# A written-out order of instructions made anew: TensorE's instruction blocks assumed to be needed later, four steps of the first chunk with other durations

## Chip, core and metric

The kernel runs on one core of a Trainium2 chip. The metric is device time in microseconds (us) of one execution, the median over runs. The profile comes from one execution, recorded by the hardware profiler; its span runs from the first to the last instruction.

## What is computed

A delta-rule attention, a recurrence over 768 positions for 4 x 8 heads of width 48, feeds a SwiGLU feed-forward layer after an RMS norm.

```python
for t in range(S):                      # S = 768, head_dim D = 48, B = 4, H = 8
    kt, vt, bt = k_n[:, :, t], v[:, :, t], beta[:, :, t, None]
    y[:, :, t] = einsum('bhd,bhde->bhe', q[:, :, t], state)
    v_old = einsum('bhde,bhd->bhe', state, kt)
    state = state + bt * einsum('bhd,bhe->bhde', kt, vt - v_old)

x = y.transpose(0, 2, 1, 3).reshape(B * S, H * D)      # 3072 tokens of 384
xn = x / sqrt(mean(x * x) + 1e-6) * rms_g
g, val = xn @ w_gate, xn @ w_val                       # 384 -> 1536
out = (silu(g) * val) @ w_out                          # 1536 -> 384
```

k_n is k divided by its norm. The weights arrive as 64-bit floats and are made into 32-bit ones on the chip.

## The kernel before

**Chunks.** The sequence is cut into 12 chunks of 64 positions (C = 64); a chunk holds 256 tokens, since all four batches go together. In a chunk the recurrence becomes dense algebra: scores of k against k, the inverse of a triangular matrix, products with the state, and an update of the state. `norms` (L604 to L632) takes the norms of k; `prep` builds the scores and the inverse, for chunks 0 and 1 in `invert` with small triangular solves on VectorE and TensorE (L701 to L882); `recur` (L1212 to L1283) solves for u, reads the output y, takes its RMS norm (for chunk 0: squares L1308, mean L1326, power L1333, products L1344 and L1348), transposes it (L1371) and multiplies it by g (L1376, L1380); the state follows from L1283. The feed-forward layer of chunks 0 and 1 is `ffn_plain`: products with w_gate and w_val at L1443, Silu at L1451, the product with it at L1452, and w_out at L1425. From chunk 2 on, `ffn` and `down` use factored products (L1538, L1595) with fewer multiplications.

**Weights.** `weights` loads 18 pieces of 768 KB each; two ScalarE steps (L500, L501) and two VectorE steps (L495, L498) make each piece into 32-bit floats. The first feed-forward products need the first pieces.

**An order written out.** Each step is recorded by `P.add(engine, duration, ...)` with what it reads and writes. `ORDER` is a long string that encodes the order in which all steps are emitted, found beforehand by a search over a model. `Plan.run` (L232) decodes it, calls `Plan.times` (L154), which gives every step a start, and emits the steps in this order. Each engine then runs its own steps in that order, whatever the real times are; semaphores keep the data right. The order on SP, the queue that issues nearly all DMAs, comes out of the same string.

**Fillers.** The model's starts have one direct effect on the program: where TensorE is expected to sit idle for over 0.8 us before 110 us, `fillers` (L104) puts in products of the identity matrix that nobody reads, of 512, 256 or 128 columns (emitted at L1714). A filler is four instructions, as is any other 32-bit product (two weight loads and two matmuls); a transpose is two.

**Instruction blocks in the model.** `times` counts TensorE's instructions. The tuple `PACKET` has three numbers: `first`, `each` and `reach` (L164). The block of number k is taken to be asked for when the count reaches first + each * k, and to be needed when it reaches that plus `reach`:

```python
first, each, reach = PACKET
...
    a, b = first + each * len(asked), first + each * used + reach
    if a >= more and b >= more:
        break
```

`fetch` (L167) gives the time at which a block is there: a lag of 4.2 us, and more when DMAs are queued. A step in which a needed block isn't there ends later by what is missing. In the kernel the numbers touch nothing else: no instruction waits because of them.

**Around the change.** In chunk 0 TensorE runs L560 (transposes of k and q), L701 (scores), L583, L842, L875, L842, L1212, L1236, L1190, L1371, L1283 and then the feed-forward layer, in this order, with fillers in between. Groups that go through 64 small products (L701, L583, L842, L875, L1212, L1236, L1190, L1283, L1113, L1128, L1176) hold 128 instructions each, except where halves are named.

Of the kernel before, what the change touches and what calls it, by code (L numbers as in the profile page):

```python
# [16 lines left out]
C = 64  # L17
W = 32
# [3 lines left out]
PACKET = (130.2, 254.45, 314.0)  # L22
# [10 lines left out]
    "#.#'#-#z#&###R#+#)#,#S#(#/#*#4#3#0#H#a#W#>#_#b#`#X#m#Y#%$:#Z#$#C$;#n#p#T#o#c#q#U#V#v#f#M#d#[#w#e#x#u#^$g#I$<#y$=#{#s"  # L33
    "#|#g#~#}#h#r#1$##t#2$$#?$l#E$%$&#]$)$($'$*$>$+#J%L$-$,#D$/$.#N#K$0#L#@%O$3#O$q$4#P%z$5$?#F$@#Q$m$7$A$6%M$B#G&$$n$o#="
    "%P$C#;#i%N#l#j$r#9#A$E#k$D$G$F$h$H$b$t$I$v$p$J$K$j%Q#8$T$L#B$M$U%y$i$V$O$W$N$1%$%[$X$Y$P%U$Z$Q$S$8$[$]$R$^%R%V&7$9${"
    "%W%S$k$d&C&8%T$s%X$c$_%)$u&9&;%Y%Z&:$e&<%](%$f&?%{#6&=%^$a&>&@%_%`$2$`%a$w&E%|'$$}%b$x&&%c&A%3&F'%%%&%%}%d#5&D&G&B%~"
    "'&&'%f&I&(%&&H$|%'&J%e%h%8$~&K%#%=%.%g%5%(&{&L&)$y%+%k&M&#%*&~&N'B%l%m%j%B%9&O%4%,%i'C&S&|%-'E$z%:%n%;%>&T&}%p%/%o%<"
    "'F%s%@%?&U%u'Q'?&*%q%6(&%t&X%r'#'D%0%A%v%G%1#7&P%2%w%x'G&Q%C&R'''H'I&Y&V'K&W('%7'J&Z'L'+%D'M&_#:((&[%H#<()&`'(')'*&]"
    "%J(*','N&a%I&+'<'R'-&b&d'.'@(z'0({&e'/'A%E(+'1'O&i%K'>'2)_&j&f&g&,&1'4%F(-&k&n'3&2'=(,)b'P*B&^'S)`&c'T'U)a&5)c'V'8&3"
    "'W&o'9'5'X':'6';)d'7'Y'Z)<)f'[)e&h&p)i'])j&m&l&4'^&6&r)h'_)g&s&q'`(6'a'b(:'c(;'d'e(7(.'f)l)k&t)+(8(<'g(9(=(/)>&x)8)?"  # L40
    "'j'h(>(|'k&u'i(}(?),)-(D(@(0(~(E's(1'u)='r(B(C(A(F'v)#)n'q)m(I'y)o'x't(G)@(J'n)p'l'p(N)q)r(K'w)s'm'z'o)t*A(O)u'{*H(L"
    ")v'|&z(P(S(2)w($*I(#'})x'~(H&y(4)y)B)z(M(Q){(3*C(X)|)A)D(Y)C*D(T*E)})~)E*F(U(Z*#*$(R(V*%,q)$(^*&(5([*G&w)](c*')F)G(_"
    ",*)H*(**(d*)).)^*+,-)/,+,p)9(W,,(`,.)0+d*7(e(a)I*0)%,/*5)&)J*1(h)'*9,0(f*3,1)1*4(i)L+f,4,<*J*8(m)K*,)2,3):,5(n,2*2)3"
    ")Q*.)M+e*6)R(])4)N*/)O)S)((j*-)P*:)T)5,7*K)6,6*;,=,x)U)V*<)W&-*L(b*?)X(o(k*=,w)Y*@+g)7*>)Z*P))+j)**N(g)[+k,8&v(p,r*M"
    ",9*R,:+h,;,>(l*S,?,s,@,A,B*T,C(q,D*U,t,E&.,F(r,u,G*V,H(s,I,J*X(w*W(t*Z+i,v(u*Y*_.Y(v*[(x*a*`*e,K.Z(y*},L*f.[+#*b*g,M"
    "*c*k.],N*h*]*i+l*d*l+$*m*^*j,O*u*n*q.^*v*Q+%,P*w+m,Q+&*x*r*~+),R*s._,S+'/G+n,T*t*O+-+o*o+(,U*y+.+/+*.`*z+5,X+0*{,V+3"
    "*p+6,W*|,y+q+7,Y+4+;/F+8.a+1+9+p+++?+r+:,b.b,),f+<+t,e+s,z+@,c+=.c,g+,);+G.d,h+A.f+C+>.e+H+y.g+D+u+z+O.h+2+v+w,],(+x"
    "+E,d,{+{+I,_+B+|.6,[+}+F+~,|,i.j+Q+J,Z+M,j,a.7+P.o,`,#+K,^.p,k.i+L-#+U,$,l+W,},o,m.8,n&/,%.9+N+X.<,&.:+R,'+S.k.l-$.m"
    "/H.n.q,~-%.r+T.s.;/N.t-'.u+V/I.>.v+[.=.w/J.x.y/K.?.z.{+]+Y.|-&+_&0.}+^-+/L.W10-)+Z.@.A+`-*.~-(11.B12/#--1z+a.C-,+c-1"
    "+b.D-.-3-213.E-7.X.F/M/$-9-8.G/%-/-O-:/&-=14-4-Q/'-5-;->-S-0-<.H/(-G-T-6-?15-H-C/)-I-R.I-J-[/*-P-D-W/+-@-U-E16-]/,-K"  # L50
    "-V-d-X/--L-Y-^//-F-M.J-Z-b17/00i/.-N-_1y-c18/O-e-f-A/91:-B.K19-h/:-g1=-j-`-i/1-n-a/8-z/=/P-k/>-o1>-l-r1E1<-{1;/Q-v1F"
    "/<-s/4-~-w/5-t-p/S-m-x-u/;-q.L/?1?.$1@-y.M0j/7.N-|.#/6.O.*/2/@.(/3.P/T0k.Q-}.R.S.&2$.T.).U.+.%1A/A/R1B..1C/D1D/E1G/C"
    "/B1H.'1I1J0o1K1L0l1M0q0p1N.,1{1O0m.V./0n1P.1/W.01|/U0r1}/X1Q1R1~/Y.-1S.2/Z1T/V1U/[.32#.5/^0s/].43c1//`/_0&0t1V3d0v/d"
    "3e0u/a/f4O/e0w/j1W/l/g/k3f1X0x0(2%/b/m1Y0*0y/c0z/p1Z0+/n1[3g/q/r/o1]/h/z2&1^/v0{/i/{1_020)3h/|2'/}1b/w0.0'0|/s/x1`0,"
    "031./~/y3i0-0:0/1c0#041a0;00080$1l051m0@0%1i093j0}0</t061o0>/u1k010=1f2)3k1q0A1p0?3?1e3l2(1n3m0D0~3@0B073n0H0E3o3p1r"
    "0F0I3q0L0P4P0J1s0C0T3x1d0M1h1#0N0O1t1$3r0G1%0K3B1&1j1v1g1'1w1(1u0V3s1)1x3A3y1*0R0U1+0Q4W0Z0S0]2*4V1,3E1-0[0^0X0W3t3F"
    "3u4Q3v3w3z0a3{0Y3|3}3~4R4#2.4$0b4S0d4%202/4&4T224'210_4(4)244*264U0`2X69230e254+6:0c272:6;0f4,0h2@0g2;2<4-6<2B2A4.2,"
    "2F2C2=2Z2G2>3C2D4/6=2P402E3G2-2H2?282Q2]412R3D2L2I2[293H6>2S2^422+2Y432_443I2M2a453J2N2`2T6?3L3K2O2e462b3M482U2g492f"
    "2V2k3N2h3O2m6@2J3P2o472W2K7&6A2l4X2n4>2p2q4B6B2w6C3Q2r6D2s2x6N6G2{6E2t2i6F2c3#3a6O4C2j2|4Y3R2y2u3$4F2}3+4E2~3%2d4G2v"
    "6I2z3'3S3-3(3,6H3&3)4D3*3b314[4Z333T3/4=347'3.4@6J4H4<306K5r4_6L3U4I6M326P4;4J6Q4A5t3V6R354?5s6S6T4N4:4K6U3W3X6V4L7."  # L60
    "3Y4M373Z6W6X366Y5x3[3]5u3^6Z3;7(383_5z3`6[4a7)3<5v3=4c7*5y4b4`6]5w4e3:4d7+4]6^5{4f6_4g6`4m4h4^4i7,5|9X8l5}5/3>4n5~39"
    "4o4j6#6a8m4u6$7-4p4s9Y6b516c4t4w6%6d8o4v4y6&6e4x536'4z4k4q8n4{6f4l6g5'684r54678p5#6h525(5;6(5$5)575*6k7/506j5+5%4|55"
    "8q5,4}6l705<6)5&568H6i715=588r5C5>5A4~5?8I6*5-5D5E5.596s5B5I5:6v5F5@6r5G8s6x6z5M5H6y6p8t5N6+5J6n5Q8v5Y6w8u6u5U729%5R"
    "8w6{5V5O8y5^5S8x5P5W5T8z6|5Z5K6m5L6o6}6,6q5`6t5X6-5[6.8J9&8|8{5_5d7#6/7$607%616~625]8K5e5g8N638L5a645b658P5f9Z668}5j"
    "8~5c9#9$9'9(779)9*5k9+8O5m9,799[78739-8M7;9]9`7:9.5h9/5l9^9a9075917=745i928Q7<93945n9_</957C5o8R;B5p8S7?5q7D8T7b7>8U"
    ";C7@7K768V967A7I7L977E7J988W7d8X;E7F7O8Y997G;D7M7P7f9:7N7Y9;;F7B7Q7H<07g7Z7U7e8Z9<7[7n7]9=7R7j7c7V9>;G7o7h7W9b7v9?7i"
    "7^8[8k9A7p7X7k;H9c7_7l9B7q7`7t7S9d8]7w7x7a9f7T7u9@7|7y9I;I7r7z9M9J8$7{8^;J7}9K9N8%8(8j9O;L9e9P;K8,9D8)7~9E848*;N8-;W"
    "9L8_;O8&;X8+;P9Q7m;M8':{8`7s8.9H8a8/9R9F:~808b9h8#9S9G:}8c9C86819W;R9T8d9V;Q82858e9U:|8:838<8f8g;%8h8i8=9j88<1;S8;;T"
    ";U8@;V<2;Y;Z87;[;]89;^;_9l8A;&;`9k8C8><38B;#;a9m;b;'<4;c;$9n;d9p8?;e;(9o;f<58D;)=u;*;@;+9q9r8E;g;,8G9v=v9s;-9x8F9w;/"
    "9|;h;.9~;0;i9}:8=x;j:#:&<79y:(;k9z:$:';19{=w::;l:%=y9t:0:):;9u:,:1;2:<9i:2:-:*:@;m:==z:3:4;n:99g:D:+:.;3:5:>:/:6;o:g"  # L70
    ":?;p={:7:E;q:A:F:J:G;u:L;A;s:K:B=|:N;t:H;4:P<8:O;r:M=}:I:Q:V=~<&>#<':Z:W>$:R:C:[>%:_:c>&:]:X>':S<9;~;5:T<#>.=Q;x:^:U"
    ":h:Y<(:`:i>(:d:a;6>):b;7;v:e;8>/;|;9:m<6:j<):f;:;;;{;<<>;=:k:n:p<$;z;>:o:s:l<%;?<:>*;}<;<<>+>,<@>->0=S>1:t:q>2<A:u>3"
    ">4>5>6<*>7<F<=<.:r>8;w<B=R;y>9<D:v>::w>c<E>;<-<,<+<G<C<L:x><:y<H:z<M=W<I>==T=Y>><R=U>?<T<S<N=X<U>@=V=Z>A<O<k=[<P=]<X"
    ">B=^<V=_<Y<Z<J>C=`<Q<c<K=a>D<m<W<d=b<o=s<e=c<n<_<f<?<p<[>b<l<s>E<`<q>F<g>G<r=d<w=t<h<y>K<x<i<a>I?y<t<]<b=e<u<z<}>H<v"
    "<^=%<j<~=#<{=&='=$=f=->X=(>Y=)=.=1>d=/=g=5?z>J=*===0=+=6=2>Z=h=3>e<|>[=4=7>U=i=,?|>S=j=8=k=;>V=>=?=l>P=m=9>W>T=:>N=n"
# [181 lines left out]
def kernel(  # L257
# [17 lines left out]
    nc = tc.nc  # L275

    B, H, S, D = q.shape
# [116 lines left out]
    P = Plan()  # L394
    V = lambda n: 0.13 + 0.0011 * n
    VF = lambda n: 0.13 + 0.0006 * n
    A = lambda n: 0.2 + 0.0008 * n
    G = lambda n: 0.15 + 0.0022 * n
# [1351 lines left out]
```

## Time and profile before

| | us |
|---|---|
| median of 3 runs | 656.71 (656.12 to 658.66) |
| the profiled execution | 654.99 |
| its span | 653.2 |
| TensorE matmul busy | 645.3 (99%) |
| VectorE busy | 540.7 (83%) |
| ScalarE busy | 300.2 (46%) |
| fillers L1714: 70 matmuls | 22.25 from their starts to the next starts |

PE is TensorE's matmul side and PEld its weight loads, which overlap; DVE is VectorE, ACT ScalarE, POOL GpSimd. In the timeline a row merges equal instructions in a row: start, duration, engine, line, operation, tiles, count, and in brackets the idle time before it and what ended it. "issue" stands for time in which the engine waited for nothing that the profile shows. In a table by stretches, the number in brackets behind an engine's busy time counts its instructions. The queue q8 of the DMA table carries TensorE's instructions.

### The profile page before, as it was taken

Reading aid. Unit: us, or ns where it says so; the run is one execution under the profiler, and the core shown is the slowest. Engines: PE = TensorE matmul, PEld = TensorE weight load, DVE = VectorE, ACT = ScalarE, POOL = GpSimd, SP = SyncE. Lnnn points to the kernel's source line nnn. Section 1 sums busy time; section 2 is a strip of 40 time slices with the busy share of each in tenths; the row PEclk is TensorE's granted clock in tenths of the full one; section 3 lists DMA queues with packets and bytes.
Section 4 is the critical chain, followed back from the end, with each engine's and each line's share of the span. In section 5 each row is a group of like instructions: output and inputs, shape, how many; then the busy total and the mean of one; then the engine's idle time right before and its main releaser. Section 6 shows DMA issues by size and latency. Waiting matters only on the chain.

```text
span 653.2 us, 23284 instructions
## 1 busy us (share of the span) xinstructions
PE 645.3 (99%) x9976; PEld 595.5 (91%) x9976; DVE 540.7 (83%) x1143; ACT 300.2 (46%) x712; POOL 137.5 (21%) x201
## 2 busy tenths in 40 slices
PE   8999999999999999999999999999999999999997
PEld 5688887788899999999999999999999999999997
DVE  6989889999899899789798798898798888558363
ACT  5778752325256344345254445345354254243231
POOL 4112250031510510510611320620510410000000
PEclk9999999999999999999999999999999999999999
DMA  9987764556656576285268385375174523111101
GB/s 213 249 241 222 216 144 71 93 84 121 145 89 99 141 142 103 51 152 114 51 107 150 53 159 102 68 153 92 47 141 80 98 59 65 21 39 25 25 1 25
DMA packets 270583, 69.36 MB, mean 106 GB/s; under 512 B 257488, under 2 KB 262736, under 8 KB 270160
## 3 DMA queue, kind: packets, MB, share of 16 engines
q1 hardware_dynamic: 269360, 67.63, 51.3%
q8 instruction: 78, 1.28, 0.8%
q10 hardware_dynamic: 1120, 0.25, 0.2%
q14 instruction: 25, 0.20, 0.1%
HBM read 49.76 MB, written 22.02 MB: 110 GB/s over the span
## 4 chain that ended last, share of the span: by engine, by line
PE 91%; SPq 3%; DMA 2%; DVE 2%; issue 1%; POOL 1%; ACT 0%; POOLq 0%; DVEq 0%; ACTq 0%
PE bank L1538 40%; PE bank L1595 20%; PE bank L1443 10%; PE bank L1425 5%; PE bank L583 3%; SPq L402 3%; PE bank L1113 3%; PE bank L1714 2%; PE bank L1190 2%; PE bank L1176 1%; PE bank L1283 1%; PE bank L1055 1%; PE bank L1075 1%; PE bank L560 1%; DMA at<-dkk 1%
## 5 line engine op out<-in xcount | busy, mean ns | idle before, releaser
L1538 PE MATMUL bank<-xf,w_in 128*128 128x128 f32 x1440 | 179.0, 276 | 0.5 <-issue 0.5
L1538 PEld LDWEIGHTS bank<-xf,w_in 128*128 128x128 f32 x1440 | 169.9, 192 | 2.1 <-issue 0.7
L1548 DVE TENSOR_TENSOR tmp<-tmp,bank 128x512 f32<-128x512 f32 x180 | 119.6, 682 | 42.9 <-PE bank L1538 33.1
L1538 PE MATMUL bank<-xf,more 128*128 128x128 f32 x960 | 124.1, 276 | 0.0
L1538 PEld LDWEIGHTS bank<-xf,more 128*128 128x128 f32 x960 | 115.4, 192 | 1.2 <-DVE tmp L1604 0.2
L1550 ACT COPY tmp<-bank 128x512 f32<-128x512 f32 x120 | 69.0, 585 | 92.3 <-PE bank L1538 53.2
L1554 ACT ACTIVATE tmp<-tmp 128x256 f32<-128x256 f32 x120 | 48.1, 416 | 63.7 <-DVE tmp L1548 63.4
L1006 DVE TENSOR_REDUCE acc<-acc 128x30 f32<-128x90 f32 (+4 forms) x150 | 71.0, 473 | 5.2
L1595 PE MATMUL bank<-wo_sb,hf 128*128 128x192 f32 x360 | 64.2, 330 | 0.0
L1000 DVE TENSOR_TENSOR acc<-acc,at 128x60 f32<-128x60 f32 (+4 forms) x150 | 53.2, 355 | 8.6 <-POOL at L980 5.5
L1595 PEld LDWEIGHTS bank<-wo_sb,hf 128*128 128x128 f32 x360 | 57.9, 190 | 1.2 <-issue 0.4
L945 POOL TENSOR_TENSOR at<-at,beta_b 128x256 f32<-128x256 f32 (+3 forms) x32 | 21.1, 693 | 156.0 <-DMA at<-dkk 156.0
L1555 DVE TENSOR_TENSOR hf<-tmp 128x256 f32<-128x256 f32 x120 | 47.1, 419 | 1.4 <-ACT tmp L1554 1.3
L628 POOL TENSOR_TENSOR knrm<-ksum,half 128x16 f32<-128x16 f32 x11 | 32.3, 2938 | 61.5 <-DVE ksum L607 61.5
L1026 POOL COPY acc<-acc 128x128 f32<-128x128 f32 x40 | 16.9, 453 | 84.5 <-DVE acc L1006 83.8
L1425 PE MATMUL bank<-wo_sb,hf 128*128 128x384 f32 x96 | 34.7, 493 | 0.0
L1443 PE MATMUL bank<-xp,w_in 128*128 128x256 f32 x144 | 34.1, 386 | 0.0
L1443 PE MATMUL bank<-xf,w_in 128*128 128x256 f32 x144 | 32.8, 382 | 0.0
L1395 DVE TENSOR_TENSOR xf<-xf 128x256 f32<-128x256 f32 (+1 forms) x70 | 28.1, 421 | 4.2 <-ACT xf L1365 3.8
L1443 PEld LDWEIGHTS bank<-xf,w_in 128*128 128x128 f32 x144 | 27.0, 190 | 4.8 <-issue 0.2
L1443 PEld LDWEIGHTS bank<-xp,w_in 128*128 128x128 f32 x144 | 26.5, 190 | 4.5 <-DVE xp L1376 0.3
L1425 PEld LDWEIGHTS bank<-wo_sb,hf 128*128 128x128 f32 x96 | 17.1, 190 | 8.4 <-issue 0.2
(221 smaller groups left out, 978.4 us busy)
## 6 DMA issues: line engine op xcount, KB each, us to landing
at<-dkk SPq DMA_DIRECT2D x20, 256.0 KB, 3.9
vt<-in_v_dram SPq DMA_DIRECT2D x24, 192.0 KB, 4.2
k<-in_k_dram SPq DMA_DIRECT2D x23, 192.0 KB, 4.5
out_dram<-tmp SPq DMA_DIRECT2D x46, 96.0 KB, 2.2
dks<-k SPq DMA_DIRECT2D x14, 256.0 KB, 3.4
kt<-dks SPq DMA_DIRECT2D x28, 128.0 KB, 3.2
more<-in_moe_w_gate_dram SPq DMA_DIRECT2D x4, 768.0 KB, 9.7
more<-in_moe_w_out_dram SPq DMA_DIRECT2D x4, 768.0 KB
```

Source lines behind the costliest of these rows:

```text
L628: P.add("POOL", 2.95, lambda: nc.gpsimd.tensor_tensor(out=knrm[i2], in0=ksum[i2], in1=half, op=ALU.pow), pn, r=[("ksum", i2), "half"], w=[ ...
L1000: nc.vector.tensor_tensor(out=acc[:, 1:3, 0:n, j + 2 : W].rearrange("p a i t -> p i a t"), in0=acc[:, old, 0:n, j : j + 2, None].to_broadc ...
L1006: nc.vector.tensor_reduce(out=acc[:, new, 0:n, j + 2 : W], in_=acc[:, lo : lo + 3, 0:n, j + 2 : W].rearrange("p a i t -> p i t a"), axis=A ...
L1395: P.add("DVE", V(128 * n), lambda dst=dst, a=a, b_=b_, op=op: nc.vector.tensor_tensor(out=dst, in0=a, in1=b_, op=op), pxv, r=[("xp", 0), ( ...
L1425: nc.tensor.matmul(po[p].t[:, 0:DM], hf[:, spot(f), 128 * p : 128 * p + 128], wo_sb[:, spot(f)], start=(f == f0), stop=(f == f1 - 1), skip ...
L1443: nc.tensor.matmul(ps.t[:, TOK * side : TOK * side + TOK], w_in[:, side, h_, 3 * t + i_, n : n + 128], x_[:, 2 * t : 2 * t + 2].rearrange( ...
L1538: nc.tensor.matmul(g.t[:, 128 * z : 128 * z + 128], fac[:, side, 128 * f : 128 * f + 128], xf[:, xs], start=(begin and z == 0), stop=False ...
L1548: P.add("DVE", V(512), lambda t=t, g=g: nc.vector.tensor_tensor(out=t, in0=t, in1=g.t, op=ALU.add), -1, r=[g], w=[tk], last=g)
L1550: P.add("ACT", A(512), lambda t=t, g=g: nc.scalar.copy(t, g.t), -1, r=[g], w=[tk], last=g)
L1554: P.add("ACT", A(256), lambda t=t: nc.scalar.activation(out=t[:, 0:256], in_=t[:, 0:256], func=ACTF.Silu), -1, w=[tk])
L1555: P.add("DVE", V(256), lambda t=t, f0=f0, p=p: nc.vector.tensor_tensor(out=hf[:, spot(f0) : spot(f0) + 2, 128 * p : 128 * p + 128], in0=t[ ...
L1595: nc.tensor.matmul(g.t[:, 0:192], a_[:, f], b_[:, f], start=(begin and f == 0), stop=(f == 5), skip_group_check=True)
```

## The change

Three edits. `reach` in `PACKET` goes from 314 to 444 instructions. In `recur`, four durations that the model uses for chunk 0 change: the squares of y (0.53 to 0.36), the scaled copy of half of y on VectorE (V(192), which is 0.34, to 0.42), and the two copies of the transposed y times g (V(128), 0.27, to 0.36 on VectorE; A(128), 0.30, to 0.37 on ScalarE). And `ORDER` is another string of the same length, so that all engines' orders, the DMAs' and the fillers change; no step is added or left out besides fillers, which go from 35 to 22.

```diff
-PACKET = (130.2, 254.45, 314.0)
+PACKET = (130.2, 254.45, 444.0)
...
 ORDER = (
-    "#.#'#-#z#&###R#+#)#,#S#(#/#*#4#3#0#H#a#W#>#_#b#`#X#m#Y#%$:#Z#$#C$;#n#p#T#o#c#q#U#V#v#f#M#d#[#w#e#x#u#^$g#I$<#y$=#{#s"
...
+    "#.#+#-#$#&###'#R#z#S#)#(#0#*#3#4#/#H#a#W#>#_#b#`#X#m#Y#,$:#Z#M$;#p#n#T#q#o#U#V#v#d#2#c#[#w#f#C#^#x#J#y#{#I#1#|#g$<#~"
...
 )
...
-                        P.add("ACT", 0.53, lambda p=p, g=g: nc.scalar.activation(
+                        P.add("ACT", 0.36, lambda p=p, g=g: nc.scalar.activation(
                             out=yn[:, p, 192 * g : 192 * g + 192], in_=psy[g, p].t[:, 192 * p : 192 * p + 192], func=ACTF.Square,
...
-                            P.add("DVE", V(192), lambda p=p, dst=dst, src=src: nc.vector.tensor_scalar(
+                            P.add("DVE", 0.42, lambda p=p, dst=dst, src=src: nc.vector.tensor_scalar(
...
-                        P.add("DVE", V(128), lambda p=p, psx=psx: nc.vector.tensor_scalar(
+                        P.add("DVE", 0.36, lambda p=p, psx=psx: nc.vector.tensor_scalar(
                             out=xdst[:, 2 + p], in0=psx.t[:, 128:256], scalar1=g_sb[:, 1:2], scalar2=None, op0=ALU.mult,
                         ), pxv, r=[psx, "g"], w=[(xkeys[p], 1)], last=psx)
                         continue
-                    P.add("ACT", A(128), lambda p=p, psx=psx, k_=k_: nc.scalar.mul(
+                    P.add("ACT", 0.37, lambda p=p, psx=psx, k_=k_: nc.scalar.mul(
```

What the new order moves on TensorE, by the built programs (counts are of its instructions, from the first filler on):

| | before | after |
|---|---|---|
| between L842 and L875 of chunk 0 | 3 fillers | 4 transposes of k (L560) |
| between L1212 and L1236 | 3 fillers, L560, 3 fillers | 2 fillers |
| between L1236 and L1190 | 3 fillers | none |
| between L1190 and L701 of chunk 1 | 3 fillers | none |
| between L701 and L1371 | L560 | L560, 3 fillers |
| between L1371 and the first L1443 | L560 | L1283, L560 |
| three 64-product groups with nothing between, counts | none | L1236, L1190, L701 at 944 to 1328; L875, L1128, L583 at 2352 to 2736; L1176, L583, L1113 at 5064 to 5448; L1113, L583, L1113 at 6436 to 6820; L1176, L1113, L1190 at 18364 to 18748 |

On POOL, the four instructions that make mask_p (L418, L421) come ahead of those that make the identity matrix. On SP, the two loads of v for chunk 0 stand between the first weight pieces instead of behind most of them, and the two loads of q for chunk 1 move ahead of loads of k, v and beta that they followed.

## The prediction

> **What bounds the kernel now.** I read the busy shares first, then who waited for whom on TensorE.
>
> ```profile
> PE 645.3 (99%) x9976; PEld 595.5 (91%) x9976; DVE 540.7 (83%) x1143; ACT 300.2 (46%) x712; POOL 137.5 (21%) x201
> q8 instruction: 78, 1.28, 0.8%
> ```
>
> TensorE (PE) is busy 99% of the span. Its instructions arrive on q8: 78 blocks, 1.28 MB, so 16.4 KB and 256 instructions each (2 x 9976 / 78).
>
> ```profile
> PE bank L1714 <- POOL ident masks.py:199: 1.4, 1, 1.4
> PE bank L669 <- DMA tmp<-in_beta_dram: 0.7, 1, 0.7
> PE bank L1714 <- issue: 0.5, 1, 0.5
> PE bank L560 <- DMA k<-in_k_dram: 0.5, 1, 0.5
> PE bank L1538 <- issue: 0.5, 1, 0.5
> ```
>
> Each line of this list of waits has a total, a number of times and the longest, in us. All data waits lie before 41 us. From the first feed-forward product on, PE never waits for data until the tail, so every us that its front takes less, and every us that it then stands still, shows in the time. Two waits are "issue", with no releaser. Where do they lie? The table by stretches, cut just before each resumes, counts the instructions that had run:
>
> ```profile
> 0.00:30.60 30.60, 27.27 (x477) 18.12 (x477) 24.07 (x70) 19.99 (x48) 8.99 (x12) 1.00 0.95 236
> 0.00:374.30 374.30, 370.14 (x6201) 326.14 (x6202) 328.94 (x710) 187.12 (x439) 96.68 (x134) 1.00 0.64 133
> ```
>
> 477 + 477 = 954 and 6201 + 6202 = 12403. The model with reach 314 puts the need of block 2 at 130.2 + 2 x 254.45 + 314 = 953.1 and of block 47 at 12403.4. Both stalls stand on a block's first instruction, to within one. With 444 the needs would be 1083 and 12533, where nothing happens. So **the trace contradicts the new number**; a program laid out by it stalls where its model sees nothing.
>
> Now the front, where the gain could be:
>
> ```profile
> 28.60 1.15 PE L1212 MATMUL bank<-vt,mt 64*64 64x48 f32 x64 [0.22 <-DVE vt L1155]
> 29.68 0.48 PE L1714 MATMUL bank<-ident 128*128 128x256 f32 x1
> 30.69 0.93 PE L1714 MATMUL bank<-ident 128*128 128x256 f32 x5 [0.52 <-issue]
> 31.45 0.60 PE L560 MATMUL bank<-ident,k 128*128 128x128 f32 x4
> 31.89 1.47 PE L1714 MATMUL bank<-ident 128*128 128x512 f32 x6
> 33.28 1.55 PE L1236 MATMUL bank<-u,kk 64*32 64x48 f32 x64
> ...
> 35.84 1.24 PE L1190 MATMUL bank<-u,pt 64*64 64x48 f32 x64
> ...
> 40.09 1.10 PE L1371 MATMUL bank<-ident,yn 128*128 128x128 f32 x6
> 41.03 0.60 PE L560 MATMUL bank<-ident,q 128*128 128x128 f32 x4
> 41.65 3.07 PE L1443 MATMUL bank<-xp,w_in 128*128 128x256 f32 x12
> 44.65 1.15 PE L1283 MATMUL bank<-u,k 64*64 64x48 f32 x64
> ```
>
> ```profile
> 30.39 0.47 ACT L1226 COPY u<-bank 128x384 f32<-128x384 f32 x1
> ```
>
> L1236 needs the copies of u, and the last ends at 30.86. It starts at 33.28: the fillers and the L560 ahead of it held it up by 2.2 us.
>
> **The change, part by part** (minus is a gain). The four durations and `reach` enter the model alone; they cost nothing but through the order.
>
> *Start.* On POOL, mask_p now precedes the identity: L418 and L421 take 0.15 and 0.79 us, with gaps 1.0. PE's first fillers start that much later; 0.52 us of it is covered by the wait for k ahead of the first L560, so the chain through L701 and VectorE's inverse starts 0.5 late. Further on, one L495 (start to start 0.47) has moved behind L1155, which releases L1212: L1212 starts at 28.6, as before. Sum 0.
>
> *From L1212 to the first L1443.* Two fillers (1.1 us) end at 30.8, u is copied by then, L1236 goes at 31.05: 2.2 earlier. L1190 follows 2.6 later, as before, at 33.6; L1371 4.3 after that, since the squares, mean, power and products between are the same, at 37.9; L1371 takes 1.1, L1283 1.1 (now ahead), L560 0.6: the first L1443 at 40.7. Before, it was 41.65 with L1283 still to do, so 42.7 for the same work: **-2.0**. Ends: -2.6, if squares and products start as early as u allows; 0, if VectorE, which by then has done two L495 and one L710 less (1.6 us), passes its arrears on.
>
> *VectorE behind it.*
>
> ```profile
> 50.00:60.00 10.00, 10.00 (x162) 7.97 (x161) 9.65 (x26) 8.66 (x17) 2.91 (x1) 1.00 0.63 159
> 60.00:70.00 10.00, 10.00 (x224) 7.95 (x223) 9.89 (x19) 7.50 (x11) 2.96 (x2) 1.00 0.97 340
> ```
>
> DVE is busy 9.65 and 9.89 of 10 us while it feeds chunk 0's products and chunk 1's inverse. A PE that is 2 us ahead meets a DVE that is 0.4 ahead (2.0 less the arrears). I take **+0.8**, half of the difference, as other products stand in between; ends 0 and 2.
>
> *Blocks.* A block is asked for 314 instructions ahead of its need. In this trace a block lands 2.05 us (fastest) to 8.6 after that, median 3.1, and the two stalls ended 1.4 and 1.5 after the landing, so it is usable 3.5 us after asking at the least, 4.5 at the median. A 64-product group takes 1.07 us for its 128 instructions (L1283 to L1443: 44.65 to 45.73), so 314 such in a row take 2.6: too short by 0.9 at least. The old order has one stretch between asking and need whose instructions alone run under 4.9 us: that of block 2, which stalled. The new order has eight:
>
> - block 9 (2420 to 2734: L875, L1128, L583): 2.6 us. DMAs are many there; blocks 8 to 10 were usable after 6.9, 4.0 and 3.9. I take 4.2: **+1.6**, ends 0.9 and 4.3.
> - block 25 (6491 to 6805: L1113, L583, L1113): 2.6. Blocks asked for in such groups past 110 us mostly come after 3.6: **+1.0**, ends 0.9 and 2.5.
> - blocks 72, 63 and 59: 3.4, 3.8 and 4.4: **+0.7** together, ends 0.1 and 3.
> - block 4 (asked for in L1190 at 34.35, needed in L1283 at 39.9): 5.5 us, against 7.0 that it took before, with SP sending four loads at 31 to 35: **+0.8**, ends 0 and 1.5. Blocks 2 and 3 have 4.8 and 5.5 us with the waits in their stretches, and few DMAs by then: 0, ends 0 and 1.
> - block 47 stalled before because it landed 4.7 us after asking; its stretch is 5.4 us of work now (5.6 before), enough for a median block: **-0.6**, ends -0.7 and 0; block 2's stall is in the front's term.
>
> Here the Trainium skill speaks for the change: "Runtime: NRT & Kernel Launch", section "Instruction fetch mechanics", has instructions streamed in 16 KiB blocks of 256, which agrees with the 16.4 KB above, and says that the fetch is hidden, because instructions are issued more slowly than blocks fill. The two waits at 954 and 12403 disagree; by that rule the block terms would be 0 and the sum -1.2.
>
> **Sum.** 0 - 2.0 + 0.8 + 1.6 + 1.0 + 0.7 + 0.8 - 0.6 = +2.3 us on a span of 653.2: 655.5. The profiled execution took 654.99 and the median is 656.71, 1.7 above it; I add 2.3 to the median: **659.0**.
>
> **Rivals.**
>
> *The blocks come in time* (the other side). Place: blocks 9 and 25. If a block were usable within 2.6 us, the stalls vanish, DVE keeps up, and the front gives 2.6: -2.6 - 0.6 = -3.2, 653.5; if all 13 fewer fillers turn to gain (4.1 us of work at 0.86, 0.43 and 0.22 us for 512, 256 and 128 columns) it is 652.0. It decides once the front gains more than the blocks cost. For it: 76 of 78 blocks caused no wait. Against: no block was usable before 3.5 us, and the old order offers no stretch as short. Chance 0.18. It is what the rule above of the Trainium skill ("Runtime: NRT & Kernel Launch") would have.
>
> *VectorE becomes the bound.* Place: L1443, L1425 and L842 between 45 and 75 us, behind L498, L1452 and L815. For it: the rows above. Against: PE never waited for DVE there, and all conversions stay in the same number. DVE keeps its time, so the whole front gain goes and the arrears of 1.6 come on top of the blocks: 2.0 + 1.6 - 0.8 = 2.8 more than the forecast, 661.8. Chance 0.16.
>
> *Slow blocks.* The stalls meet queued DMAs: block 5 took 8.6 us to its landing before, block 71 8.3. Blocks 9, 4 and the three others at their upper ends: 2.7 + 0.7 + 2.3 = 5.7 more, 664.7. For it: DMA share 0.97 between 60 and 70 us. Against: the median. Chance 0.24. The Trainium skill, "TensorE: Matmul & The Clock Gate", Part 1, adds that the clock halves after an idle window of some 3.4 us; no run here shows that for a stall, and the 0.8 us gap at 374 had full-rate matmuls behind it.
>
> **How the numbers follow.** The forecast has 0.42, with its own range 656.5 to 662. A difference under 0.5%, 3.3 us, is about what a measurement of this kernel can't tell from none: 653.4 to 660.0 is "same". Forecast: 0.31 same, 0.11 slower; blocks in time: 0.10 faster, 0.08 same; VectorE: 0.06 same, 0.10 slower; slow blocks: 0.24 slower. Faster 0.10, same 0.45, slower 0.45. Range 654.0 to 665.5: the rivals' times, and a little of the upper ends together.
>
> **What would show it.** In the waits of TensorE: "issue" ahead of L583 near 75 us after some 2734 instructions and of L1113 near 6805, 0.9 us or more each, resuming 1.4 after a q8 landing. The first L1443 at 40 to 41 with L1283 ahead of it; fillers 22. Waits of PE for DVE between 45 and 75 would show the VectorE rival. I am wrong in the mechanism if PE passes 2734 and 6805 without an issue wait, and in the front if the first L1443 stands past 42.

## The result, and the profile after

The changed kernel took 666.23 us (median of 4 runs, 665.70 to 667.96); the kernel before took 657.25 in the 4 runs it is compared with (656.12 to 658.66). The ratio is 1.014, with a 95% interval of 1.011 to 1.017: slower by some 9 us, where +2.3 was forecast and 665.5 was the upper end of the range. The profiled execution took 665.91 us, its span is 664.2, 11.0 more than the profile of before, which was one of the quicker executions of that kernel (654.99 us).

The busy shares and the granted clock, from the page of after:

```profile
PE 648.7 (98%) x9950; PEld 597.1 (90%) x9950; DVE 546.4 (82%) x1143; ACT 297.8 (45%) x712; POOL 137.4 (21%) x201
PEclk8989999999999999999999999999999999999999
```

TensorE has 26 matmuls fewer (13 fillers of two each) and is busy 3.4 us longer; in the first slices its clock is no longer full. So part of the loss does not show as idle time at all. The rest is in the list of who waited for whom on TensorE in after (total, times, longest):

```profile
PE bank L1113 <- issue: 2.2, 2, 1.7
PE bank L1714 <- POOL ident masks.py:199: 2.2, 1, 2.2
PE bank L1283 <- issue: 1.4, 2, 1.2
PE bank L583 <- issue: 1.3, 1, 1.3
PE bank L842 <- issue: 1.3, 1, 1.3
...
PE bank L875 <- ACT kt L572: 0.7, 1, 0.7
```

Before had 1.0 us of waits on "issue" in two places; after has 6.2 in six. Where they stand, and what the clock does around them, is read from the table by stretches of after (stretch, its length, then busy time and count of PE, PEld, DVE, ACT and POOL, the granted clock, the DMA share and GB/s):

```profile
0.00:82.80 82.80, 73.58 (x1367) 55.30 (x1368) 67.25 (x161) 54.37 (x116) 17.12 (x21) 0.94 0.85 217
0.00:214.20 214.20, 203.16 (x3404) 163.75 (x3404) 185.71 (x403) 111.08 (x259) 49.94 (x61) 0.98 0.69 154
26.73:30.14 3.41, 2.18 (x77) 1.72 (x74) 3.27 (x8) 3.41 (x6) 0.00 (x0) 1.00 0.67 212
30.14:33.55 3.41, 3.20 (x119) 3.20 (x118) 1.42 (x2) 0.94 (x2) 0.00 (x0) 0.50 1.07 268
211.05:214.46 3.41, 1.72 (x108) 1.60 (x100) 3.38 (x10) 0.18 (x2) 0.00 (x0) 1.00 0.60 115
214.46:217.87 3.41, 3.41 (x29) 2.93 (x27) 3.41 (x7) 1.66 (x5) 1.19 (x2) 0.50 0.54 127
```

1367 + 1368 = 2735 and 3404 + 3404 = 6808 instructions had run when L583 and L1113 resumed: blocks 9 and 25, by the prediction's formula at 2734.3 and 6805.5. The last four rows show the clock: behind a stretch of 3.41 us in which TensorE worked 2.18 or 1.72 us, the next stretch is granted half the clock. Three such rows (from 13.08, 30.14 and 33.55) lie in the front, one at 214.46.

The front on TensorE in after (start, time, instruction, idle time before it), and below it two rows of before from the same place:

```profile
12.89 6.81 PE L1714 MATMUL bank<-ident 128*128 128x512 f32 x14
19.62 1.16 PE L583 MATMUL bank<-qt,kt 64*64 64x64 f32 x64
...
28.37 0.73 PE L842 MATMUL bank<-mt,m1bd 64*64 64x32 f32 x9
30.35 1.61 PE L842 MATMUL bank<-mt,m1bd 64*64 64x32 f32 x52 [1.25 <-issue]
31.68 0.32 PE L1212 MATMUL bank<-vt,mt 64*64 64x48 f32 x1
...
33.73 2.50 PE L1714 MATMUL bank<-ident 128*128 128x512 f32 x4
36.16 1.91 PE L1236 MATMUL bank<-u,kk 64*32 64x48 f32 x64
38.80 1.38 PE L1190 MATMUL bank<-u,pt 64*64 64x48 f32 x64 [0.73 <-DVE u L1250]
...
43.83 1.01 PE L1283 MATMUL bank<-u,k 64*64 64x48 f32 x51
46.07 0.44 PE L1283 MATMUL bank<-u,k 64*64 64x48 f32 x13 [1.23 <-issue]
...
46.93 3.40 PE L1443 MATMUL bank<-xp,w_in 128*128 128x256 f32 x15
```

```profile
11.86 4.47 PE L1714 MATMUL bank<-ident 128*128 128x512 f32 x14
16.27 1.16 PE L583 MATMUL bank<-qt,kt 64*64 64x64 f32 x64
```

The first L1443 starts at 46.93 with L1283 done. Before, that point is 42.7 (41.65, and 1.07 for the L1283 that follows). So 4.2 of the 11.0 us are lost up to there and 6.8 behind it. Of the 6.8, 4.0 are idle time (gaps of over 0.15 us) that before does not have, and at most 1.7 the half-speed row at 214.46; in the rest, L583 and L1113 take some 1.4 us longer in sum, which was not followed further. The four matmuls of two fillers (L1714) take 2.50 us here; they took 1.35 at full clock in the run e2 below.

### The profile page after: what moved, and what is told of

Its sections match the earlier page's. It is cut to its first block, busy times and chain, and to the rows that moved or that the text cites. A ratio compares the mean times of both kernels' runs of the same rounds, so it can differ in the third digit from the quotient of the medians.

```text
span 664.2 us, 23263 instructions
## 1 busy us (share of the span) xinstructions
PE 648.7 (98%) x9950; PEld 597.1 (90%) x9950; DVE 546.4 (82%) x1143; ACT 297.8 (45%) x712; POOL 137.4 (21%) x201
## 4 chain that ended last, share of the span: by engine, by line
PE 92%; DVE 3%; issue 1%; ACT 1%; DMA 1%; SPq 1%; POOL 0%; DVEq 0%; POOLq 0%; ACTq 0%
PE bank L1538 41%; PE bank L1595 21%; PE bank L1443 9%; PE bank L1425 4%; PE bank L583 3%; PE bank L1113 3%; PE bank L1190 2%; PE bank L1176 2%; PE bank L1283 1%; PE bank L1714 1%; DMA beta_b<-in_beta_dram 1%; PE bank L1075 1%; PE bank L1055 1%; SPq L402 1%; PE bank L842 1%
## 5 line engine op out<-in xcount | busy, mean ns | idle before, releaser
L1538 PE MATMUL bank<-xf,w_in 128*128 128x128 f32 x1440 | 179.3, 276 | 0.1
L1538 PEld LDWEIGHTS bank<-xf,w_in 128*128 128x128 f32 x1440 | 169.5, 192 | 1.7 <-issue 0.6
L1548 DVE TENSOR_TENSOR tmp<-tmp,bank 128x512 f32<-128x512 f32 x180 | 119.8, 680 | 41.7 <-PE bank L1538 28.4
L1538 PE MATMUL bank<-xf,more 128*128 128x128 f32 x960 | 123.3, 276 | 0.0
L1538 PEld LDWEIGHTS bank<-xf,more 128*128 128x128 f32 x960 | 115.1, 192 | 1.0
L1595 PEld LDWEIGHTS bank<-wo_sb,hf 128*128 128x128 f32 x360 | 59.2, 193 | 1.4 <-issue 0.6
L1555 DVE TENSOR_TENSOR hf<-tmp 128x256 f32<-128x256 f32 x120 | 48.5, 421 | 3.4 <-ACT tmp L1554 2.9
L1443 PE MATMUL bank<-xp,w_in 128*128 128x256 f32 x144 | 33.6, 383 | 0.0
L1443 PE MATMUL bank<-xf,w_in 128*128 128x256 f32 x144 | 33.0, 382 | 0.0
L1395 DVE TENSOR_TENSOR xf<-xf 128x256 f32<-128x256 f32 (+1 forms) x70 | 30.0, 457 | 2.6 <-ACT xf L1365 2.1
L1443 PEld LDWEIGHTS bank<-xp,w_in 128*128 128x128 f32 x144 | 26.7, 190 | 6.0 <-DVE xf L495 1.6
L1443 PEld LDWEIGHTS bank<-xf,w_in 128*128 128x128 f32 x144 | 27.0, 190 | 4.6
L1425 PEld LDWEIGHTS bank<-wo_sb,hf 128*128 128x128 f32 x96 | 17.5, 190 | 9.1 <-issue 0.4
```

Of the source, the lines that this page charges most:

```text
L1395: P.add("DVE", V(128 * n), lambda dst=dst, a=a, b_=b_, op=op: nc.vector.tensor_tensor(out=dst, in0=a, in1=b_, op=op), pxv, r=[("xp", 0), ( ...
L1425: nc.tensor.matmul(po[p].t[:, 0:DM], hf[:, spot(f), 128 * p : 128 * p + 128], wo_sb[:, spot(f)], start=(f == f0), stop=(f == f1 - 1), skip ...
L1443: nc.tensor.matmul(ps.t[:, TOK * side : TOK * side + TOK], w_in[:, side, h_, 3 * t + i_, n : n + 128], x_[:, 2 * t : 2 * t + 2].rearrange( ...
L1538: nc.tensor.matmul(g.t[:, 128 * z : 128 * z + 128], fac[:, side, 128 * f : 128 * f + 128], xf[:, xs], start=(begin and z == 0), stop=False ...
L1548: P.add("DVE", V(512), lambda t=t, g=g: nc.vector.tensor_tensor(out=t, in0=t, in1=g.t, op=ALU.add), -1, r=[g], w=[tk], last=g)
L1555: P.add("DVE", V(256), lambda t=t, f0=f0, p=p: nc.vector.tensor_tensor(out=hf[:, spot(f0) : spot(f0) + 2, 128 * p : 128 * p + 128], in0=t[ ...
```

## The experiments

All have the line numbers of the two kernels. A block's stretch is the work between the request for it and its first instruction. The request is the kernel's own model (130.2 + 254.45 k instructions); the traces show when a block moves and lands, and in the fifteen of them none moved sooner than 0.8 us after its request so counted. To keep the fillers from being planned anew, each pins them to those of before or of after; that edit is the same everywhere and is shown once, with `{...}` for the list of one of the two kernels:

```diff
-                if op.fill:
-                    filler(op.fill, spare[-1][1])
+                if op.n in (FILL := {...}):
+                    filler(FILL[op.n], spare[-1][1])
```

Orders are strings, so their edits are given by line. Ratios are to the kernel before, run on the same chip, 5 rounds each.

**Front and rest apart.** e1 has the old front and the new rest, e2 the reverse.

```diff
 # e1_old_front
-ORDER = (order of after)
+ORDER = (order of before up to the third L1443, the steps left in the order of after)
 # e2_new_front
-ORDER = (order of before)
+ORDER = (order of after up to the first L1443, the steps left in the order of before)
```

> The order of before up to the third L1443 of the front, the order of after behind it, the fillers of before. Theory (two separate losses, front +4.2 us and +6.8 us behind it, each made by its own order): the front is that of before (first L1443 near 42 with the 0.5 us wait on an issue near 30), and the waits on issue before L583 near 78 us (1.3 to 1.6) and before L1113 near 209 us (1.7 to 2.0, with a half-speed clock row behind it) are still there: +5 to +6.5 us on the span of 653.2, ratio to before 1.008 to 1.010. Rival (the later losses are arrears that the late front hands on, on VectorE): without the late front they go too, ratio 1.000 to 1.003. Rival (the later order is the whole loss): ratio 1.013 or more.

> The order and fillers of after up to the first L1443, the order of before behind it. Theory: the front's loss alone. First L1443 with L1283 behind it in the account at 46.5 to 47.3, three granted-clock rows of 0.5 before 37 us, waits on issue before L842 and L1283; behind it none of 1 us or more, as no stretch of less than 4.1 us of work lies between a block's request and its need: +3.5 to +4.5 us, ratio 1.005 to 1.007. Rival (arrears handed on): later waits of PE for VectorE or ScalarE between 45 and 80 us, ratio 1.010 or more. Rival (the front's loss is won back by an engine that meanwhile gets ahead): ratio 1.000 to 1.003.

e1: ratio 1.0071 (1.0049 to 1.0093), span 658.7. e2: 1.0082 (1.0051 to 1.0113), span 659.5. Over the span of before these are 5.5 and 6.3 us, together 11.8 for the 11.0 of the whole change: two separate losses. e1 is a little below the range that was expected for it; the half-speed row that was expected in it does not stand there. TensorE's waits in e1:

```profile
PE bank L1190 <- issue: 1.3, 1, 1.3
PE bank L1113 <- issue: 1.1, 2, 0.7
...
PE bank L583 <- issue: 0.7, 1, 0.7
```

The wait before L583 (block 9), one of those before L1113 (block 25) and the one before L1190 (block 72) are there with the old front too, the first two shorter than after's and the third longer; the clock stays full. In e2, TensorE's timeline of the front:

```profile
29.96 0.23 PE L1212 MATMUL bank<-vt,mt 64*64 64x48 f32 x1
...
32.41 0.28 PE L1236 MATMUL bank<-u,kk 64*32 64x48 f32 x4
34.53 1.47 PE L1236 MATMUL bank<-u,kk 64*32 64x48 f32 x60 [1.85 <-issue]
...
37.91 0.30 PE L701 MATMUL bank<-kt 64*64 64x64 f32 x4
41.00 1.98 PE L701 MATMUL bank<-kt 64*64 64x64 f32 x60 [2.79 <-issue]
```

L1236 starts 2.45 us after L1212, where it took 4.68 in before: this is the gain that the prediction counted. Four matmuls later TensorE waits 1.85 us for block 2, and then 2.79 for block 3. These are not the waits that were expected (L842 and L1283, three half-speed rows): there is one such row, at 41.03, and the first L1443 stands at 47.58. Behind the front e2 shows two waits for data (L1113 for ScalarE's state 1.6, L842 for VectorE 0.7), at 58 and 77 us. They are the sign that was given for the rival "arrears handed on", in a smaller size, and the ratio, 1.0082, lies above the range that the theory gave, 1.005 to 1.007.

**Three groups in a row.** A group of this kind has 64 matmuls and 64 weight loads, 128 instructions; where the texts speak of 64 small products, these 64 matmuls are meant, two of which make a 32-bit product. e3 sets the groups at blocks 9 and 25 apart; e4 leaves the order and moves the boundaries.

```diff
 # e3_apart, on TensorE
-L1443, L1443, L875, L1128, L583, L1443, L1425
+L1443, L875, L1443, L1128, L1425, L583, L1443
-L1595, L1055, L1113, L583, L1113
+L1055, L1113, L583, L1595, L1113
 # e4_shift
+            [self.ops[63].fn() for _ in range(3 if op.n == 322 else 0)]
             op.fn()
```

> After with three steps moved by a few places, so that the three adjacent groups of 64 small products that fill block 9's stretch, and the three of block 25's, no longer stand in a row; the same fillers and the same number of instructions. Theory (a block that is asked for some 315 instructions ahead comes too late where those are all quick): no wait on issue of 1 us or more before L583 near 82 us nor before L1113 near 213 us, and no half-speed clock row at 214.5; 1.5 + 1.9 + 1.7 = 5.1 us less than after, up to 0.6 of it given back at block 25, whose stretch is 4.4 us now: ratio 1.006 to 1.008. Rival (the gaps there are a wait for data or an engine that the profile names wrongly): the same three groups wait as long wherever they stand, ratio 1.012 to 1.016.

> After with 36 small products (three more times the products of L642, into a bank that is written again) ahead of the L1443 that precedes block 9's three groups: the steps keep their order, and every later block boundary falls 144 instructions earlier in them. The added products take 2.5 us (24 such matmuls took 0.85). Theory (where a block's first instruction falls decides, not the step): no wait on issue of 1 us or more in L583 near 85 us and in L1113 near 215 us, and a new one of 0.9 to 1.9 us near 175 us in L1113 or L583, at block 20, whose stretch now is L1176, L583 and L1113, 2.6 us of work; 2.5 - 1.5 - 3.6 - 1.0 (blocks 64 and 72) + 1.4 + 0.4 = 1.8 us less than after, ratio to before 1.008 to 1.013. Rival (the gaps belong to those steps and their data): they stay, and the products come on top, ratio 1.016 to 1.019.

e3: ratio 1.0138 (1.0096 to 1.018), span 661.9, 2.3 less than after and not 5.1; the interval alone says nothing. The waits on issue at blocks 9 and 25 are gone, and the half-speed row at 214 with them. But TensorE's waits in e3 have a new one:

```profile
PE bank L875 <- DVE x2bd L833: 2.0, 1, 2.0
```

L875 starts at 77.43 in e3 and at 77.91 in after, though e3 was ahead by then: it waits for VectorE, which is late by as much, and a half-speed row (79.12 to 82.54) follows that wait. So the removed 5.1 us were given back in part, 1.3 by a longer wait and up to 1.7 by the clock. e3 bears out the theory on what makes the waits, and not on what they are worth.

e4: ratio 1.0247 (1.0216 to 1.0279), above both expectations. Its front, which is after's, was slower by itself (first L1443 at 48.12, half clock from 36.26 to 46.50), and blocks 8, 9, 20 and 32 made it wait 0.5, 1.4, 2.0 and 1.0 us. What it was made for is the row of its table by stretches that ends in the new wait, and TensorE's timeline there:

```profile
0.00:177.40 177.40, 164.28 (x2766) 128.00 (x2767) 148.28 (x323) 91.80 (x209) 43.96 (x53) 0.96 0.69 164
```

```profile
174.78 0.73 PE L1113 MATMUL bank<-state,qt 48*64 48x48 f32 x34
177.48 0.68 PE L1113 MATMUL bank<-state,qt 48*64 48x48 f32 x30 [1.97 <-issue]
```

2766 + 2767 = 5533, block 20 by the formula (130.2 + 20 x 254.45 + 314 = 5533.2), in a row of groups that did not wait in after. The wait in L583 is gone and stands in L1128, 144 instructions earlier; the one at 213 is gone. The waits follow the boundaries, not the steps. The expected saving at block 9 was wrong: its request then fell behind slow transfers (7.3 us to the landing).

**The same in the old order.** e7 was to put L1176, L1113 and L1190 into block 66's stretch. One L1538 there came ahead of the L1548 on VectorE that was still to read the bank it writes, so the result is not that of before; and L1190 waited 0.8 us for VectorE just where the block landed. Nothing follows from it. e9 does it in two other places.

```diff
 # e7_stall_in_old, TensorE near 530 us: three L1538 moved ahead of L1176, L1113 and L1190
 # e9_two_stalls, TensorE near 265 and 360 us
-L1176, L1113, L1595, L1538, L1190
+L1176, L1113, L1190, L1595, L1538
-L1055, L1113, L1075, L1595, L1595, L1176, L1113
+L1055, L1113, L1113, L1075, L1595, L1595, L1176
```

> Before with three steps moved late in the kernel (near 530 us), so that L1176, L1113 and L1190, three groups of 64 small products, stand in a row exactly between the request for block 66 and its first instruction; nothing else differs. Theory: a wait on issue of 1.2 to 2.0 us before L1190 there, and where the clock is then granted at half, up to 1.7 us more: +1.2 to +3.7 us, ratio 1.002 to 1.006. Rival (the same three groups in a row cost nothing, fetching of instructions is hidden, and the gaps in after have another cause): ratio 0.999 to 1.001 and no wait on issue.

> Before with two steps moved by two and by four places, far behind the front: one L1190 ahead of an L1595, so that L1176, L1113 and L1190 fill the stretch from the request for block 33 to its first instruction (2.6 us of work), and one L1113 ahead of an L1075, so that L1055, L1113 and L1075 do so for block 45 (2.9 us). Theory: two new waits on issue, 0.9 to 1.9 us before L1190 near 265 us and 0.6 to 1.6 us before L1075 near 360 us, and 0 to 1.7 us for each where the granted clock falls: +1.5 to +5 us, ratio 1.002 to 1.008. Rival (fetching is hidden, and the gaps in after have another cause): no wait on issue there, ratio 0.999 to 1.001.

e7: ratio 0.9995 (0.9969 to 1.002). e9: 1.0017 (0.9994 to 1.0041), which leaves the expected 1.002 open at its lower end; the trace decides. TensorE in e9:

```profile
268.28 0.76 PE L1190 MATMUL bank<-u,pt 64*64 64x48 f32 x37
270.50 0.61 PE L1190 MATMUL bank<-u,pt 64*64 64x48 f32 x26 [1.46 <-issue]
...
366.10 0.43 PE L1595 MATMUL bank<-wo_sb,hf 128*128 128x192 f32 x1
367.34 1.89 PE L1595 MATMUL bank<-wo_sb,hf 128*128 128x192 f32 x10 [0.81 <-issue]
```

Up to 270.45, 8842 instructions had run (block 33: 8841.1), up to 367.15 11898 (block 45: 11894.5). Two moves of a few places make two waits, 2.3 us in all, in a kernel that has nothing else of the change. The second wait stands one matmul behind the L1075 for which it was expected. The blocks landed 1.5 and 1.3 us before TensorE resumed. No half clock followed.

e15 does the reverse at block 47, where before has a wait.

```diff
 # e15_block47, TensorE near 372 us
-L1190 and L1283 (one step), L1538, L1538
+L1538, L1538, L1190 and L1283 (one step)
```

> Before with one L1190 (of 256 instructions) two places later, behind two L1538, so that block 47's stretch has 6.7 us of work and not 5.3; nothing else differs. Theory: the wait on issue of 0.5 to 0.8 us near 374 us is gone and none takes its place; 0.4 to 0.8 us less, which the times can hardly tell: ratio 0.997 to 1.001. Rival (the wait belongs to the L1538 there): it stays.

Its list of waits has no "issue" at all, and block 47 landed 3.8 us before its need. The ratio is 1.000 (0.9981 to 1.002): half a us can't be seen in the times. With it a wait of before was taken away without another in its place, and still no version here was measurably faster than before.

All fifteen traces together leave no other place for these waits: they hold 51 waits of TensorE on issue of over 0.15 us, and each of them ends within five instructions of a block's first instruction by the formula with 314.

**What the front loses, by engine.** e8 tests the prediction's gain in the old front, e12 the fillers in the new, e10, e11 and e14 exchange the order of single engines, and e5 one step of VectorE.

```diff
 # e8_fewer_fillers: before, list of fillers
-224: [2, 1, 1], 123: [4, 1, 1],
 # e12_fillers_back: e2 with the list of before
 # e10_old_loads: e2, SP in the order of before
 # e11_new_loads: before, SP in the order of e2
 # e14_old_pe_order: e2, TensorE in the order of before and with its fillers
 # e5_inverse_later: after, VectorE
-L631, L632 (chunk 1), ... L815 x2 (chunk 0)
+... L815 x2 (chunk 0), L631, L632 (chunk 1)
```

> Before without the six fillers that stand between L1212 and L1236 (0.86, 0.43, 0.22 us: 2.6 us of TensorE's work); the order stays. The prediction's own step put the first L1236 2.2 us earlier for it and the first L1443 2.0. That rival: first L1236 near 31.0, first L1443 near 39.5 to 40, ratio 0.996 to 0.998. Theory (blocks 2 and 3 come when they come, and the fillers filled the time until then): the waits on issue before 41 us grow from 0.5 us to 1.5 to 2.7, the first L1443 stands 0 to 1 us earlier at most, or later if a granted-clock row falls to 0.5: ratio 0.998 to 1.003.

e8: ratio 1.0026 (1.0004 to 1.0048), so the time that the rival, the prediction's own step, gave is out. TensorE in e8:

```profile
30.38 1.15 PE L1212 MATMUL bank<-vt,mt 64*64 64x48 f32 x64 [0.22 <-DVE vt L1155]
32.12 0.66 PE L560 MATMUL bank<-ident,k 128*128 128x128 f32 x4 [0.59 <-DVE kk L853]
32.70 1.55 PE L1236 MATMUL bank<-u,kk 64*32 64x48 f32 x64
...
41.91 2.42 PE L1443 MATMUL bank<-xp,w_in 128*128 128x256 f32 x9 [0.20 <-ACT xp L1380]
```

L1236 comes 2.3 us after L1212, and the first L1443 11.5 after it, 1.5 less than in before: most of the 2.0 is there, more than the theory allowed, and the waits on issue before 41 us are still 0.5 us, where the theory had 1.5 to 2.7. So in the old front the six fillers did cost time, and the theory falls there. The gain does not last. Block 8, whose boundary the missing fillers moved, then costs 1.1 us of idle at 72, and the median ends above before's; the whole of that difference is not accounted for.

> The run e2_new_front with the fillers of before (13 more, 4.1 us of TensorE's work at full clock). The prediction counted fewer fillers as time gained. Theory (the fillers stood where TensorE has to wait for blocks and data anyway): the waits on issue before 47 us shrink from 4.6 us to 2.5 or less, the first L1443 stays within 1.2 us of e2's 47.6, ratio to before 1.006 to 1.010. Rival (fillers cost what they take): first L1443 near 51, ratio 1.012 to 1.015. Rival (the clock: more fillers keep it at full speed): no granted-clock row of 0.5 before 50 us and the first L1443 at 46 or earlier, ratio 1.003 to 1.006.

e12: 1.0112 (1.0071 to 1.0153). The waits on issue before 48 us are 3.3 us (4.6 in e2), the first L1443 is 1.1 later. So 4.1 us of fillers cost 1.1 in the front, as the theory had it, but the waits shrank less than it said, and the ratio lies above its range. They did not keep the clock either (half from 34.41 to 37.82).

> The run e2_new_front with SP's loads sent in the order of before; TensorE, VectorE, ScalarE and POOL keep the new front's order. In the new fronts so far block 1 (asked for at 19.2 to 20.6 us) began to move 5.5 to 8.2 us after the request and block 3 (30.0 to 32.9) 3.1 to 8.6 after, with a 768 KB load sent at 15 and two at 32 to 36; in the old fronts block 3 began 2.2 to 3.7 after the request. Theory (loads sent just ahead of a request keep the block back): block 3 begins within 4.5 us of its request, the waits on issue before 47 us are 1.5 us in all or less (e2: 4.6), the first L1443 stands at 43.5 to 45.5, ratio to before 1.000 to 1.004. Rival (the order of the products alone makes the stretches too short): 3 to 5 us of waits on issue, first L1443 at 46.5 to 48, ratio 1.006 to 1.010. Rival (the loads moved because their users moved): waits of VectorE and PE for data take the place, ratio 1.004 or more.

> The other half: before with SP's loads of the front sent in the order of after; the order on all other engines and the fillers are those of before. Theory (loads ahead of a request): block 1 begins to move 5.5 us or more after its request and block 3 six or more, waits on issue of 1.5 to 4 us before 41 us, ratio 1.003 to 1.007. Rival (the order of products): waits on issue near 0.5 us as in before, ratio 0.999 to 1.002, unless a conversion on VectorE or ScalarE waits for a load that is now later (a wait for DMA data would show it).

> The run e2_new_front with TensorE's order and fillers of before; VectorE, ScalarE, POOL and SP keep the order of after in the front. Theory (TensorE's order alone makes the stretches of blocks 2, 3 and 4 too short): waits on issue of 0.4 to 1.2 us in all before 47 us (e2: 4.6), first L1443 at 42 to 44.5 with L1283 still to do, no granted-clock row of 0.5 behind a wait on issue, ratio to before 1.000 to 1.004; a data wait may stand where the other engines now do something else first. Rival (the other engines' order and loads make the blocks late): waits on issue of 2 us or more, ratio 1.006 to 1.010.

| | first L1443, L1283 done | waits on issue before 48 us | ratio, interval |
|---|---|---|---|
| before (profile) | 42.7 | 0.5 | |
| e11: only SP new | 45.9 | 1.1 | 1.0053, 1.0026 to 1.0079 |
| e14: all new but TensorE | 45.8 | 0.7 | 1.0048, 1.0033 to 1.0063 |
| e10: all new but SP | 48.2 | 5.8 | 1.0075, 1.0047 to 1.0103 |
| e2: all new | 47.6 | 4.6 | 1.0082, 1.0051 to 1.0113 |

The loads in the old order take no wait away (e10): that theory falls. TensorE in its old order takes 3.9 of the 4.6 us of waits on issue away (e14), and its time falls between the two expectations. What is left in e14 is waits for data, by its list:

```profile
PE bank L1714 <- POOL ident masks.py:199: 2.2, 1, 2.2
PE bank L583 <- ACT qt L572: 1.8, 1, 1.8
PE bank L1714 <- issue: 0.7, 1, 0.7
```

In e11 too most of the loss is a wait for data (L842 for ScalarE's mt, 2.3), not for blocks: ScalarE stands still 4.34 us, 0.20 in before, for a weight piece that SP now sends later, and the step that makes mt (L822) is behind it. This is the exception that the rival named. So the new front costs in two ways: TensorE's order through the blocks, and the other engines' order through data. By the ratios they are worth about 0.003 and 0.005; the first difference is no larger than its interval, the waits themselves are plain. The exchanges do not add up: the loads alone cost 0.005 (e11), and putting them back wins nothing that can be told (e10).

In e14 block 3 took 6.6 us from request to landing, as long as in after's fronts (4.4 to 9.5), but its stretch lasted 8.3 us there. What makes blocks 1 to 4 so slow in these fronts is not settled. Over the fifteen traces, a block began to move 1.5 us (median) after the request where other transfers filled under 15% of the DMA engines in the two us behind the request, and 3.0 where they filled over 95%; one in ten took over 6.8 there.

> After with one step moved on VectorE: the square root and reciprocal of chunk 1's norms (L631, L632) stand behind the L815 of chunk 0 and not ahead of it; so POOL's scaling of k (L894), which they release, starts later. In the four profiles so far, L815 x2 took 1.97 us where L894 ran on POOL at the same time, and 0.76 where it did not. Theory (the two share something and VectorE waits): L815 x2 takes 0.76 us, the first L842 starts 1.0 to 1.4 earlier after L815's start, and the time is 0 to 1.3 us shorter than after's, as far as the waits on issue behind it don't take the gain back: ratio 1.011 to 1.014. Rival (L815 takes 1.97 because of its operands): 1.97 again and no change but the delay of the norm.

e5: ratio 1.0131 (1.0101 to 1.0161), as after. VectorE and POOL in after, and then in e5:

```profile
21.91 1.97 DVE L815 TENSOR_TENSOR mt<-acc,side 128x256 f32<-128x256 f32 x2
...
22.13 1.47 POOL L894 TENSOR_TENSOR k<-k,krec 128x768 f32<-128x768 f32 x1 [2.83 <-DVE krec L632]
```

```profile
21.38 0.76 DVE L815 TENSOR_TENSOR mt<-acc,side 128x256 f32<-128x256 f32 x2
...
23.36 1.48 POOL L894 TENSOR_TENSOR k<-k,krec 128x768 f32<-128x768 f32 x1 [4.40 <-DVE krec L632]
```

Without POOL's L894 beside it, L815 takes 0.76 us again: the second of the pair had stood still until L894 was done. The expected 1.2 us at L842 did not come, as L842 follows 4.95 us after L583 in both, which is its fillers and products: TensorE was late anyway, and VectorE's loss lay behind it. The Trainium skill, "SBUF — State Buffer", section "SBUF: two separate sides", says that VectorE and GpSimd share a pair of ports under an exclusive lock, and names operations with two inputs in that memory; both runs agree.

## Why the prediction was wrong

Its mechanism held, that a block's first instruction waits where its request came too late, and the model with 444 sees nothing of it. Its sum failed in the front. In the two profiles the front, up to the first L1443 with L1283 done, is 4.2 us longer, where the terms for it gave -1.2; behind it the terms gave +3.5, and it is 6.8. By its own sign, a first L1443 past 42, it was wrong in the front.

*Start: 0.* L1212 started at 31.68 and not at 28.6. L583 was 3.35 late, most of it from the half-speed row at 13.08: the seven fillers that run there took 6.81 us and not 4.47; 1.5 came back, as five fillers and not eight stand between L583 and L842 (the table ahead of the prediction leaves that place out); then block 1, which was not on the list of blocks, made TensorE wait 1.25. In the seven runs with the new order on TensorE and VectorE L1212 starts at 29.3 to 31.7, in the six with the old front at 28.3 to 30.5, 0.8 less on average. So over the runs the step is off by less than in these two profiles; the one of before was quick here (L583 at 16.27; 18.0 to 18.1 in e8, e9 and e15, behind a half-speed row at 11 to 15).

*From L1212 to the first L1443: -2.0. This is the step that failed, with the blocks that "Blocks" took at nothing here: 2 and 3 at 0, and 1 not listed.* The distance was to be 12.1 us, where the old front takes 14.1 with L1283. It was 15.25 in after, and 15.5 to 18.9 in e2, e3, e4, e5 and e10. In after, 1.23 of this is the wait for block 4, which has its own term. The rest went between L1212 and L1236, which are 4.48 us apart and not 2.45: the clock is half from 30.14 to 36.97, behind the wait for block 1, and the sum had no term for that. Blocks 2 and 3 cost nothing in after, since TensorE came to them late, 9.0 and 7.1 us after their requests. In the other five runs L1236 does come 2.4 us after L1212, and the gain is lost to blocks 2 and 3 instead, 2.5 to 4.6 us together. The prediction saw stretches of 4.8 and 5.5 us for them, "and few DMAs by then". In e2 TensorE came to them 5.1 and 7.6 us after the requests, which is no less; but they landed 5.3 and 8.9 us after the requests, where the prediction reckoned with a median of 3.1, and DMAs were not few. A row of e2's table by stretches:

```profile
30.00:34.00 4.00, 2.68 (x88) 1.91 (x81) 3.79 (x7) 2.81 (x5) 0.00 (x0) 1.00 1.11 219
```

The DMA share is 1.11 there, 0.80 between the same times in before; whether that alone made the blocks slow stays open. So the term for the products was sound, and what was taken at nothing, the blocks on their way and the clock behind a wait for one, was larger than the gain.

*Block 4: +0.8.* 1.23 of idle in after; within its ends.

*Block 9: +1.6, block 25: +1.0.* 1.3 and 1.7 of idle, at the instructions foretold, resuming 1.5 and 1.7 us after the landings (81.37 and 212.61). Block 25 also lost the clock for 3.41 us, up to 1.7 more: the prediction had no term for it. It weighed a half clock only behind an idle window of some 3.4 us, by the Trainium skill ("TensorE: Matmul & The Clock Gate", Part 1). The window's length agrees, 3.41 us on a fixed grid; that it must be idle does not.

*Blocks 72, 63 and 59: +0.7.* 0.1 of idle at 72, none on PE at the others; blocks 64 and 16, which weren't named, cost 0.5 and 0.2. *Block 47: -0.6.* Its wait is gone, as foretold.

*VectorE: +0.8.* One wait, L875 before 77.9, 0.7, put down to ScalarE. The size is right, by luck: e3 shows VectorE late there by 2.0 once TensorE no longer waits for blocks. So the rival "VectorE" is real in e3, and in after it was covered.

The forecast's direction was right. The rival "slow blocks" (664.7) came nearest, but it placed its cost at blocks 9, 4 and later, and in after blocks 9 and 4 cost 1.32 and 1.23, near what the forecast gave them; the time went to block 1, block 25 and the clock. That it came near is luck. The rule of the Trainium skill that instruction fetch is mostly hidden ("Runtime: NRT & Kernel Launch", "Instruction fetch mechanics"), under which the kernel would have been faster, does not hold here: e9 makes 2.3 us of waits by it alone.

## What to carry to other kernels

Before a filler or a wait is counted as gain, ask what else arrives during it: in e2 the instruction blocks of the next 314 instructions did, and the time came back as waits from four matmuls later on. It need not be so: in e8 1.5 of the 2.0 us stayed, up to the first L1443. What is shown here is where the waits stand and why; that removing one gives its time back is not (e3). A planner's constant that the trace contradicts must not be changed to fit: count the instructions up to each wait on issue, set the model by that count, and look for stretches that are all small products between a request and its need. And a small stall can cost more than its length, when the clock is lost behind it.

## What was not expected of the hardware

The granted clock is set anew on a fixed grid of 3.413 us (in after the half-speed rows begin at 13.08, 30.14 and 214.46, 5 and 54 such stretches apart). In the fifteen traces here (the first 6 us and the end left out), each of the ten stretches of the grid in which TensorE was busy less than 55% was followed by one at half clock; of the 44 between 55% and 75%, 11 were; of the more than 2700 above, one, which was itself at half clock. So a stall of 1.2 to 2 us may or may not cost the clock, as it falls into one stretch or across two: in after 1.69 us of idle at 213 lay in one, left it 50% busy, and did; in e4 1.97 us at 176 fell across two, 80% and 63% busy, and did not.

In the 51 waits on issue TensorE resumed 1.2 to 2.0 us after the landing, and no sooner than 3.2 us after the request (block 25 in e1); the prediction's 3.5 was near.
